# A decode layer: twelve down-projection chunks in one load, and TensorE's waits for itself moved to the other buffer

## The chip, the core and the metric

The kernel runs on one core of a Trainium2 chip. The core has five engines that run their own instruction streams: TensorE (PE; its weight loads are shown apart as PEld), VectorE (DVE), ScalarE (ACT), GpSimd (POOL) and SyncE (SP). Sixteen DMA engines carry data between HBM and the on-chip memory (SBUF). Engines tell one another through semaphores. The metric is the device time of one execution in microseconds (us), as the median of several runs. The profile is one more execution; its times are counted from the first instruction of the span.

## The reference

One token for each of eight sequences goes through an attention layer with a window of 1024 cached positions and a gated feed-forward layer, all in float32:

```python
h  = x + A(_layernorm(x))     # A: q = x @ wq; softmax(q k^T * Dh**-0.5) @ v over the last 1024
                              #    positions; 32 query heads on 4 key/value heads; then @ wo
h2 = h + B(_layernorm(h))     # B: (gelu(x @ w_gate) * (x @ w_up)) @ w_down
```

The width is 1024, the inner width of the feed-forward layer 3584. With eight tokens there is little arithmetic for each weight; weights and cache are 111 MB, and each byte is used once.

## The kernel before

**Stream.** All weights and both caches lie in HBM in the order in which they are used. SP issues them as one queue of loads into two SBUF buffers, `wbuf[0]` and `wbuf[1]`, each of 64 KB on each of the 128 partitions. Loads 0 to 11 fill one whole buffer each, in turn: 8 MiB, one row of 64 KB for each partition. Buffer 0 gets the even loads, buffer 1 the odd ones. `flow` lists them; `load(k, clear)` on L182 to L187 issues one, and L394 to L397 give each load its wait: the buffer has to be free, which TensorE tells by the semaphore `steps`.

**TensorE's loop.** TensorE runs a loop of stages. One pass is: eight transposes (`transposes`, L129), the sixteen products of buffer 0's first half, the sixteen of its second half, eight transposes, then the same two halves of buffer 1 (`products(i, half)`, L135 to L153). The text names these steps as the code does: t0, a0, a1, t1, b0, b1, with the pass in brackets, so b1(5) is the second half of buffer 1 in pass 5. There are passes 0 to 5, and pass 6 has t0, a0 and a1 alone. Each step ends by counting `steps` up by one. `pe(pass, step)` is the wait for that.

**One product** takes a 128x32 stationary tile and 512 columns of a weight row block. Its 32 outputs go to one of four strips of PSUM partitions (`j` = 0 to 3), and `c` = 0 to 3 accumulates. Products with different `j` can run side by side on the array; the profile has two MATMUL records for each product.

**The waits of TensorE for its own count.** In `products`, L150 to L152, TensorE counts up the semaphore `pace` with a product and at once waits for that count. So it waits until that product has ended before it begins the next. Before the change this is done in the second half of buffer 0, after the products 1, 3 and 5, in every pass.

**The end of the stream.** Load 11 carries the last up-projection columns and chunks 0 to 7 of the down projection (a chunk is 128 rows of `w_down`, 4 KB on each partition). Load 12 has chunks 8 to 15 in the first half of buffer 0 (32 KB rows), loads 13 and 14 have four chunks each in its second half (16 KB rows). Load 12 tells of its landing by the buffer's semaphore `landed[0]`; loads 13 and 14 have one of their own, and L418 and L419 let GpSimd pass each landing on to TensorE, as the release of products 0 to 7 and of 8 to 15 of a1(6). Two more loads bring chunks 24, 25 and chunk 26 into buffer 1, and two last ones chunk 27 in two column blocks (160 and 96 of each 256); they wait for b0(5) only.

**What is done with them.** b1(5) multiplies chunks 0 to 7, a0(6) chunks 8 to 15, a1(6) chunks 16 to 23. VectorE sums the parts in `d0` (L440, L442). TensorE then multiplies chunks 24 and 25 (L448), adds `d0` into the same accumulator by two constant matrices (L455), multiplies chunk 26, and ScalarE copies the sum to `s_sb` (L461). The two blocks of chunk 27 (L467) are added to it by VectorE (L470), and two DMAs store the result.

Of the kernel before, what the change touches and what calls it, by code (L numbers as in the profile page):

```python
# [10 lines left out]
D = 1024  # L11
# [5 lines left out]
NQ = 4  # L17
# [5 lines left out]
HALF = BUF // 2  # L23
# [2 lines left out]

LATE = (5, 6, 4)

PARTS = (8, 8, 4, 4, 2, 1)
ENDS = (160, 96)  # L30
SINGLES_AT, LAST = 24, 27

# [1 line left out]
class Flow:  # L34
# [38 lines left out]
    def run(self, engine, make, *waits, mark=True):  # L73
        ins = self.start(engine, make, waits)
        if not mark:
            return None
        self.done[engine] += 1
        ins.then_inc(self.own[engine], 1)
        return self.own[engine], self.done[engine]
# [6 lines left out]
    def go(self, engine, sem, n, *waits):  # L86

        self.start(engine, lambda e: e.sem_inc(sem, n), waits)


def decode_block(nc, x, flow, tail, outs):

    fl = Flow(nc)
    run, move, go = fl.run, fl.move, fl.go
# [18 lines left out]
    ready = [fl.sem("ga"), fl.sem("gb")]  # L113
# [5 lines left out]
    def pe(it, step):  # L119
        return steps, 6 * it + 1 + ("t0", "a0", "a1", "t1", "b0", "b1").index(step)  # L120
# [5 lines left out]
    def take(sem, n):  # L126
        t.wait_ge(sem, n).then_inc(sem, -n)  # L127
# [7 lines left out]
    def products(i, half):  # L135
        if half == 0:
            take(landed[i], 16)
        take(ready[i], 1)
        out = big[i][:, half * N:(half + 1) * N]
        for n in range(4 * NQ):  # L140
            c, j = divmod(n, NQ)
            if (i, half, n) == (0, 1, 8):
                take(ready[i], 1)
            s0 = (half * NQ + j) * WIN + 32 * c
            w0 = half * HALF + (c * NQ + j) * N
            ins = t.matmul(  # L146
                out[32 * j:32 * j + 32, :], st[i][:, s0:s0 + 32], wbuf[i][:, w0:w0 + N],
                start=(c == 0), stop=(c == 3))

            if (i, half) == (0, 1) and n in (1, 3, 5):  # L150
                ins.then_inc(pace, 1)
                take(pace, 1)  # L152
        ins.then_inc(steps, 1)  # L153
# [3 lines left out]
    with nc.body("stage", valid_engines=[PE]):  # L157
        back = t.mark_branch_hint_location()
        transposes()
        products(0, 0)  # L160
        products(0, 1)
        nc.br_cmp(count, 6, on_true="rest", on_false="down", comp_op="IS_LT", engines=[PE])
    with nc.body("rest", valid_engines=[PE]):
        transposes()
        products(1, 0)
        products(1, 1)
        t.reg_add(count, count, 1)
        t.br_lt(count, 7, on_true="stage", on_false="down").branch_hint(back)
# [13 lines left out]
    def load(k, *waits):  # L182
        i, a, src, own = flow[k]
        n = src.shape[1]
        s = fl.sem(f"part{k}") if own else landed[i]
        fl.start("sync", lambda e: e.dma_start(wbuf[i][:, a:a + n], src), waits).then_inc(s, 16)
        return s, 16  # L187
# [63 lines left out]
    def paired(engine, i, k, src, *waits):  # L251

        s = src.rearrange("p (c e) m -> p e c m", e=2)
        for e2 in range(2):
            tok = run(engine, lambda e: e.tensor_copy(  # L255
                windows(i)[:, k, 2 * e2:2 * e2 + 2].rearrange("p h (c m) -> p h c m", m=32),
                s[:, e2].unsqueeze(1).to_broadcast([P, 2, 4, 32])), *waits)
        return tok
# [6 lines left out]
    for hf in range(2):  # L265
# [9 lines left out]
        for s in range(2):  # L275
# [5 lines left out]
        fill = run("gpsimd", lambda e: e.tensor_copy(  # L281
            st[hf].rearrange("p (k n) -> p k n", k=2),
            qz[hf].unsqueeze(1).to_broadcast([P, 2, NQ * WIN])), tok, pe(0, end))
# [30 lines left out]
    for hf in range(2):  # L314
# [23 lines left out]
        for s in range(2):  # L338
            fill = paired("gpsimd", hf, s, ot[:, s * REP:(s + 1) * REP].rearrange(
                "p h b r -> p h (b r)"), tok, pe(2, ("a1", "b1")[hf]))  # L340
# [40 lines left out]
    fill = paired("gpsimd", 1, 0, xt.rearrange("p c b r -> p c (b r)"), b_free, pe(4, "b1"))  # L381
# [11 lines left out]
    arrived = {}  # L393
    for k in range(2, len(flow)):  # L394
        i, a, src, mine = flow[k]
        clear = pe(k // 2 - 1, ("a1", "b1")[i]) if k < 12 else pe(5, "a0" if k == 12 else "a1")
        arrived[k] = load(k, clear)  # L397

    fill = paired("gpsimd", 1, 1, at[:, 0:8], at_ok[0], b_free)
# [14 lines left out]
    fill = paired("gpsimd", 0, 0, at[:, 8:16], at_ok[0], a_free, pe(5, "a1"))  # L414
    go("gpsimd", ready[0], 1, fill)
    at_ok.append(to_chunks(16, len(LATE), pe(6, "t0")))
    fill = paired("gpsimd", 0, 1, at[:, 16:24], at_ok[1], pe(5, "a1"))
    for k in (13, 14):  # L418
        go("gpsimd", ready[0], 1, fill, arrived[k])  # L419


    later = wbuf[1][:, 0:HALF]
# [2 lines left out]
    for k, src in enumerate(tail[:-len(ENDS)]):  # L425
        n = src.shape[1] // D
# [129 lines left out]
```

## Time and profile before

| | before |
|---|---|
| median of 3 runs | 264.21 us (264.13 to 264.34) |
| the profiled execution | 263.94 us |
| its span, first to last instruction | 262.6 us |
| PE busy / PEld busy | 152.1 us / 51.7 us |
| DVE, ACT, POOL busy | 34.7, 16.6, 16.0 us |
| DMA | 111.31 MB, mean 424 GB/s over the span |
| mean granted TensorE clock | 0.825 |

The profiled execution is 1.3 us longer than its span, for what lies around the first and the last instruction. In the rows that follow, a row of the timeline is: start, duration, engine, line, operation, tiles, shapes, count, and in brackets the idle time before it. A row of the waits or of the DMA issues names the engine that waits or issues. A "q" behind an engine (SPq, PEq) is its sequencer.

### The profile page before, as it was taken

To read this page: it belongs to the slowest core of one execution; us is meant where nothing else is said; L and a number is where in the kernel's file an instruction comes from. 1 tells how busy PE (TensorE), PEld (TensorE's weight loads), DVE (VectorE), ACT (ScalarE), POOL (GpSimd) and SP (SyncE) were. 2 spreads that over 40 slices of the span, in tenths; PEclk is the share of its full clock that TensorE was granted. 3 is DMA by queue.
4 is the path that set the end of the run, shared out by engine and by line. 5 is a ranking of instruction groups with operands and counts; after the bars stand their busy time and mean duration, and the time that the engine had idled before them with its cause. 6 is when DMAs were issued, how large, how long until landed. Compare 5 with 4: busy or idle time off the path is not lost. (4 is left out here: it accounts for less than half of the span.)

```text
span 262.6 us, 2312 instructions
## 1 busy us (share of the span) xinstructions
PE 152.1 (58%) x984; PEld 51.7 (20%) x984; DVE 34.7 (13%) x78; ACT 16.6 (6%) x25; POOL 16.0 (6%) x31
## 2 busy tenths in 40 slices
PE   0024955805937827917618928429909609809976
PEld 0021221301222222212112212122302202302312
DVE  0220010100021110040310020730100300201211
ACT  1000000000030020000000000300200000000000
POOL 5020010010000000020020000020000110100100
PEclk9999995975975956995975977956985967977999
DMA  8998997999899799989979998997999899799995
GB/s 319 484 419 379 479 479 329 469 479 429 369 479 479 339 459 479 439 359 479 479 329 469 479 429 369 479 479 329 469 479 439 359 479 479 329 464 404 422 417 220
DMA packets 3056, 111.31 MB, mean 424 GB/s; under 512 B 480, under 2 KB 736, under 8 KB 1008
## 3 DMA queue, kind: packets, MB, share of 16 engines
q1 hardware_dynamic: 2880, 111.23, 98.4%
q10 hardware_dynamic: 176, 0.08, 0.1%
HBM read 111.18 MB, written 0.13 MB: 424 GB/s over the span
## 5 line engine op out<-in xcount | busy, mean ns | idle before, releaser
L146 PE MATMUL big<-w,st 128*32 128x512 f32 x832 | 132.2, 720 | 73.8 <-PEq L127 72.1
L146 PEld LDWEIGHTS big<-w,st 128*32 128x32 f32 x832 | 36.4, 129 | 161.4 <-issue 158.9
L132 PE MATMUL tp<-ident,tin 128*128 128x128 f32 x104 | 17.5, 323 | 34.2 <-PEq L127 34.2
L132 PEld LDWEIGHTS tp<-ident,tin 128*128 128x128 f32 x104 | 14.0, 166 | 44.5 <-issue 44.5
L255 POOL COPY st<-ot 128x256 f32<-128x256 f32 x8 | 2.9, 400 | 77.1 <-DVE ot L334 77.1
L293 DVE TENSOR_REDUCE nmax<-big 128x1 f32<-128x1024 f32 x2 | 2.4, 1224 | 30.7 <-PE big L146 30.7
L246 POOL COPY st<-xt 128x1024 f32<-128x1024 f32 x2 | 3.0, 1524 | 52.2 <-DVE xt L241 52.2
L271 DVE TENSOR_TENSOR tin<-big,q 128x512 f32<-128x512 f32 x2 | 1.4, 692 | 31.3 <-PE big L146 31.3
L319 DVE TENSOR_TENSOR o<-big,o 128x512 f32<-128x512 f32 x2 | 1.4, 692 | 28.6 <-PE big L146 28.6
L255 POOL COPY st<-at 128x256 f32<-128x256 f32 x6 | 2.8, 494 | 36.0 <-DVE at L385 18.5
L281 POOL COPY st<-qz 128x1280 f32<-128x1280 f32 x2 | 2.5, 1254 | 34.1 <-DVE qz L276 34.1
L270 ACT COPY q<-big 128x512 f32<-128x512 f32 x2 | 1.2, 586 | 34.5 <-PE big L146 34.5
L255 POOL COPY st<-xt 128x256 f32<-128x256 f32 x2 | 1.3, 660 | 31.8 <-DVE us L377 31.8
L348 DVE TENSOR_TENSOR y<-big,y 128x512 f32<-128x512 f32 x1 | 0.7, 692 | 18.4 <-PE big L146 18.4
L318 ACT COPY o<-big 128x512 f32<-128x512 f32 x2 | 1.2, 585 | 28.9 <-PE big L146 28.9
L404 DVE TENSOR_TENSOR gs<-big,gs 128x512 f32<-128x512 f32 x1 | 0.7, 691 | 17.4 <-PE big L146 17.4
L295 ACT ACTIVATE tin<-big,nmax 128x1024 f32<-128x1024 f32 x2 | 2.2, 1114 | 11.9 <-DVE nmax L293 11.9
L295 ACT ACT_TABLE_LOAD x1 | 1.3, 1283 | 26.8 <-DVE nmax L293 26.8
L226 ACT ACT_TABLE_LOAD x2 | 2.6, 1283 | 1.9 <-POOL ident L197 1.9
L442 DVE TENSOR_TENSOR d<-big,d 128x512 f32<-128x512 f32 x2 | 1.4, 692 | 9.5 <-PE big L146 9.5
L373 DVE TENSOR_TENSOR gs<-big,gs 128x512 f32<-128x512 f32 x1 | 0.7, 692 | 14.6 <-PE big L146 14.6
L403 ACT COPY gs<-big 128x512 f32<-128x512 f32 x1 | 0.6, 585 | 30.6 <-PE big L146 30.6
(69 smaller groups left out, 42.4 us busy)
## 6 DMA issues: line engine op xcount, KB each, us to landing
w<-weights SPq DMA_DIRECT2D x1, 4096.0 KB, 23.7
w<-weights SPq DMA_DIRECT2D x2, 2048.0 KB, 24.7
w<-weights SPq DMA_DIRECT2D x1, 1024.0 KB, 16.1
w<-weights SPq DMA_DIRECT2D x1, 512.0 KB, 17.0
w<-weights SPq DMA_DIRECT2D x1, 320.0 KB, 17.3
w<-weights SPq DMA_DIRECT2D x12, 27.9
w<-weights SPq DMA_DIRECT2D x1, 192.0 KB, 17.3
out<-o_fin SPq DMA_DIRECT2D x1, 80.0 KB, 1.7
```

What stands on the lines that cost most here:

```text
L132: ins = t.transpose(tp[:, i * P:(i + 1) * P], tin[:, i * P:(i + 1) * P], ident)
L146: ins = t.matmul(out[32 * j:32 * j + 32, :], st[i][:, s0:s0 + 32], wbuf[i][:, w0:w0 + N], start=(c == 0), stop=(c == 3))
L226: tok = run("scalar", lambda e: e.activation(sd, ve, AF.Sqrt), tok)
L246: fill = run(engine, lambda e: e.tensor_copy(windows(i), half.unsqueeze(2).to_broadcast([P, 2, NQ, 4 * 32])), tok, *clear)
L255: tok = run(engine, lambda e: e.tensor_copy(windows(i)[:, k, 2 * e2:2 * e2 + 2].rearrange("p h (c m) -> p h c m", m=32), s[:, e2].unsqueez ...
L270: tok = run("scalar", lambda e: e.copy(q_sb, w0), pe(0, ("a0", "b0")[hf]))
L271: tok = run("vector", lambda e: e.tensor_add(tin[:, 0:N], w1, q_sb), tok, pe(0, end), pe(0, ("t0", "t1")[hf]))
L281: fill = run("gpsimd", lambda e: e.tensor_copy(st[hf].rearrange("p (k n) -> p k n", k=2), qz[hf].unsqueeze(1).to_broadcast([P, 2, NQ * WIN ...
L293: tok = run("vector", lambda e: e.tensor_reduce(out=nmax, in_=s_ps, axis=AX.X, op=ALU.max, negate=True), pe(1, ("a1", "b1")[hf]))
L295: p_ok = run("scalar", lambda e: e.activation(tin, s_ps, AF.Exp, bias=nmax, accum_out=tot), tok, pe(1, ("t0", "t1")[hf]))
L319: tok = run("vector", lambda e: e.tensor_add(o_sb, big[hf][:, N:2 * N], o1), tok, pe(2, ("a1", "b1")[hf]))
L442: tok = run("vector", lambda e: e.tensor_add(d0, ya[:, k], d0), tok, pe(6, f"a{k}"))
```

## The change

Three things are done. The row blocks of the down projection are cut into parts of 8, 12, 4, 2 and 1 chunks in place of 8, 8, 4, 4, 2 and 1: chunks 8 to 19 come as one load of 48 KB rows, which covers the first half of buffer 0 and half of its second half. This load waits for a1(5), as the next one does, where the old load 12 waited for a0(5) alone. The release of products 0 to 7 of a1(6) no longer waits for a landing of its own. And TensorE's waits for its own count are taken out of the second half of buffer 0 and put into the second half of buffer 1, after the products 1, 3, 5, 7, 9, 11 and 13: seven in each of passes 0 to 5, where there were three in each of passes 0 to 6.

```diff
-PARTS = (8, 8, 4, 4, 2, 1)
+PARTS = (8, 12, 4, 2, 1)
...
-            if (i, half) == (0, 1) and n in (1, 3, 5):
+            if (i, half) == (1, 1) and n % 2 == 1 and n < 4 * NQ - 1:
                 ins.then_inc(pace, 1)
                 take(pace, 1)
...
-        clear = pe(k // 2 - 1, ("a1", "b1")[i]) if k < 12 else pe(5, "a0" if k == 12 else "a1")
+        clear = pe(k // 2 - 1, ("a1", "b1")[i]) if k < 12 else pe(5, "a1")
...
-    for k in (13, 14):
-        go("gpsimd", ready[0], 1, fill, arrived[k])
+    go("gpsimd", ready[0], 1, fill)
+    go("gpsimd", ready[0], 1, fill, arrived[13])
...
-    flow += [(0, HALF + m * 4 * D, srcs[13 + m], True) for m in range(2)]
-    decode_block(nc, x=aps["x"], flow=flow, tail=srcs[15:], outs=outs)
+    flow.append((0, HALF + 4 * D, srcs[13], True))
+    decode_block(nc, x=aps["x"], flow=flow, tail=srcs[14:], outs=outs)
```

TensorE's rows for the second half of buffer 0, as the difference has them ("ga" is the semaphore that releases buffer 0's products, "pace" the one for TensorE's own count):

```order
 L146 MATMUL big<-w,st 32x512 x15
 L146 MATMUL big<-w,st 32x512 [waits ga_done]
-L146 MATMUL big<-w,st 32x512
-L146 MATMUL big<-w,st 32x512 [waits pace_done]
-L146 MATMUL big<-w,st 32x512
-L146 MATMUL big<-w,st 32x512 [waits pace_done]
-L146 MATMUL big<-w,st 32x512
-L146 MATMUL big<-w,st 32x512 [waits pace_done]
-L146 MATMUL big<-w,st 32x512
+L146 MATMUL big<-w,st 32x512 x7
 L146 MATMUL big<-w,st 32x512 [waits ga_done]
 L146 MATMUL big<-w,st 32x512 x7
```

The three waits are gone; the wait for the release of the last eight products stays where it was.

The end of TensorE's loop before, from the last fifteen products of b0 on ("gb" releases buffer 1's products; L167 and L168 count the pass and branch back):

```order
L146 MATMUL big<-w,st 32x512 x15
L146 MATMUL big<-w,st 32x512 [waits gb_done]
L146 MATMUL big<-w,st 32x512 x15
L167 REGISTER_ALU
L168 COMPARE_AND_BRANCH
```

The last seven rows of the same place now:

```order
L146 MATMUL big<-w,st 32x512
L146 MATMUL big<-w,st 32x512 [waits pace_done]
L146 MATMUL big<-w,st 32x512
L146 MATMUL big<-w,st 32x512 [waits pace_done]
L146 MATMUL big<-w,st 32x512
L167 REGISTER_ALU
L168 COMPARE_AND_BRANCH
```

These are the last two of the seven waits; the fifteen products that ran without one now go two at a time, up to the branch.

SP's queue before, from load 2 on ("steps" is TensorE's count of finished steps; a row without a wait follows a row that has waited for the same):

```order
L186 DMA w<-weights 128x16384 [waits steps_done] x10
L186 DMA w<-weights 128x8192 [waits steps_done]
L186 DMA w<-weights 128x4096 [waits steps_done]
L186 DMA w<-weights 128x4096
L83 DMA w<-weights 128x2048 [waits steps_done]
```

And now:

```order
L186 DMA w<-weights 128x16384 [waits steps_done] x10
L186 DMA w<-weights 128x12288 [waits steps_done]
L186 DMA w<-weights 128x4096
L83 DMA w<-weights 128x2048 [waits steps_done]
L83 DMA w<-weights 128x1024
```

One load fewer is issued, and the remaining one of 128x4096 no longer has a wait of its own, since the load ahead of it already waits for a1(5).

## The prediction

> **What bounds the kernel now.** I read the DMA queues first, since the kernel uses each byte once, then the windows in time order, the chain that ended last, and the timeline of TensorE from the landing of load 11 on.
>
> ```profile
> span 262.6 us, 2312 instructions
> q1 hardware_dynamic: 2880, 111.23, 98.4%
> 40.00:80.00 40.00, 22.87 (x144) 7.97 (x144) 3.12 (x7) 3.52 (x5) 1.25 (x1) 0.76 1.00 431
> 234.00:258.00 24.00, 20.02 (x143) 5.70 (x147) 3.90 (x6) 1.17 (x2) 1.14 (x2) 0.88 0.97 414
> 235.89 5.64 PE big L146 x32
> 242.39 17.33 DMA w<-weights
> ```
>
> In the windows the last two numbers are the DMA engines' share and GB/s. SP's one queue is busy for 98.4% of sixteen engines' span. It runs at 431 GB/s in mid kernel and at 414 at the end, where rows get short; there are no pauses to win back. In the chain the last 17.33 us before the final products are the queue's. So time goes only if the stream or the little behind it gets shorter. It comes if the stream stops, or if TensorE is still at work when the last bytes land. The second is the question here.
>
> **TensorE beside the end of the stream, before.**
>
> ```profile
> 235.89 9.03 PE L146 MATMUL big<-w,st 128*32 128x512 f32 x64 [7.11 <-PEq L127]
> 244.85 1.09 PE L132 MATMUL tp<-ident,tin 128*128 128x128 f32 x8
> 245.87 3.64 PE L146 MATMUL big<-w,st 128*32 128x512 f32 x32
> 250.43 1.05 PE L146 MATMUL big<-w,st 128*32 128x512 f32 x4 [0.92 <-PEq L127]
> 251.63 1.05 PE L146 MATMUL big<-w,st 128*32 128x512 f32 x4
> ...
> 255.30 1.92 PE L146 MATMUL big<-w,st 128*32 128x512 f32 x16 [0.21 <-PEq L127]
> 257.74 1.07 PE L448 MATMUL acc<-w,at 128*32 128x256 f32 x16 [0.52 <-DMA w<-weights]
> 258.60 0.64 PE L448 MATMUL acc<-d,add 128*32 128x256 f32 x8
> 259.03 0.64 PE L448 MATMUL acc<-w,at 128*32 128x256 f32 x8
> ```
>
> In order: b0(5) with b1(5), t6, a0(6), the paced pairs of a1(6), its second half, then the final chunks. TensorE waits between them: 0.92 us for load 13, 0.21 for load 14, 0.52 for chunks 24 and 25. That is its spare time.
>
> **Price of a self-wait.** Two products between waits come every 251.63 - 250.43 = 1.20 us. Unpaced products:
>
> ```profile
> 241.30 0.14 PEld L146 LDWEIGHTS big<-w,st 128*32 128x32 f32 x4 [0.29 <-issue]
> 241.73 0.14 PEld L146 LDWEIGHTS big<-w,st 128*32 128x32 f32 x4 [0.29 <-issue]
> ```
>
> Four records, which are two products, go every 0.43 us. So a wait costs 1.20 - 0.43 = 0.77 us of TensorE: two strips of the array stand empty.
>
> **Part 1, waits out of buffer 0.** Three waits go in each pass: 3 x 0.77 = 2.3 us earlier at the end of a1. Passes 1 to 6 gain that only on TensorE. The next thing a1 releases is a load that queues behind the other buffer's.
>
> **Part 2, waits into buffer 1.** Before, b1(5) has eight groups from 241.30 on, the last at 241.30 + 7 x 0.43 = 244.31, and ends at 235.89 + 9.03 = 244.92. Now its last pair begins at 241.30 + 7 x 1.20 = 249.70 and ends at 250.75. So b1 ends 5.8 us later, in each of passes 0 to 5. Two things are behind it in TensorE's queue: t0 of the next pass, and a0 behind that. SP's next odd load waits for it too.
>
> *Does the stream stop?* The closest odd loads:
>
> ```profile
> 206.85 0.33 SPq L186 DMA_DIRECT2D w<-weights  x1
> 189.65 0.33 SPq L186 DMA_DIRECT2D w<-weights  x1
> w<-weights SPq DMA_DIRECT2D x1, 26.6
> out<-o_fin SPq DMA_DIRECT2D x1, 80.0 KB, 1.7
> ```
>
> Load 11, issued at 206.85, would go at 212.65. Load 10 ahead of it lands at 189.65 + 26.6 = 216.25. How long an issue takes to bring its first bytes isn't shown for a large load. It is above zero, and at most 1.7 us by the nearest row, an idle queue's store from issue to landing. I take 1.7; that leaves 3.6 - 1.7 = 1.9 us, so I cost it at nothing. The other odd loads are issued at the same place of a pass. If the cover were gone, each us beyond it would cost one us in each of five passes.
>
> *Do the passes fall behind?* The dependent step closest to its landing is a0(4), behind the second layer norm, t0(4) and VectorE's fill:
>
> ```profile
> 174.34 0.69 DVE L246 COPY st<-xt 128x1024 f32<-128x1024 f32 x1
> 177.84 1.08 PE L146 MATMUL big<-w,st 128*32 128x512 f32 x4 [4.06 <-PEq L127]
> ```
>
> The fill ends at 175.03 + 5.8 = 180.8, so a0(4) begins 3.0 us late, and a1(4) gets 2.3 back. Load 10 goes at 189.65 + 0.7 = 190.4. Its 8.4 MB take 19.5 us at 431 GB/s, so load 9 has the queue until 216.25 - 19.5 = 196.8. Hidden.
>
> *At the end it is not hidden.* b1(5) starts after load 11's landing, which nothing here moves. So:
> - t6 begins at 244.85 + 5.8 = 250.7, a0(6) at 251.7.
> - a0(6) and a1(6) run without waits: sixteen groups of 0.43, and 0.63 more for the last one (3.64 - 7 x 0.43): 251.7 + 15 x 0.43 + 0.63 = 258.8. Before, a1(6) ended at 255.30 + 1.92 = 257.2. It ends **1.55 us later**, after the three waits of a1(6) have been given back.
>
> ```profile
> 246.60 1.14 POOL L255 COPY st<-at 128x256 f32<-128x256 f32 x2 [17.06 <-DVE at L385]
> 257.28 0.69 DVE L442 TENSOR_TENSOR d<-big,d 128x512 f32<-128x512 f32 x1 [7.01 <-PE big L146]
> 259.73 0.37 ACT L461 COPY s_sb<-acc 128x256 f32<-128x256 f32 x1 [14.16 <-PE acc L448]
> 260.38 0.33 DVE L470 TENSOR_TENSOR o_fin<-yt,s_sb 128x160 f32<-128x160 f32 x1 [2.40 <-PE yt L467]
> ```
>
> - a1(6)'s stationary tiles, filled by POOL, would be ready at 247.74 + 5.8 = 253.6; a1(6) needs them at 255.1. Hidden.
> - L442's second addition begins at 258.85 and ends at 259.54, so the products with `d0` begin at 259.6 in place of 258.60: 1.0 us late. Chunks 24 and 25 go ahead of them, from 258.6 to about 259.5, so they don't bind.
> - Chunk 26 follows 0.43 later and ends at 260.67; `s_sb` is there at 260.73 + 0.37 = 261.1. The final addition begins at 261.15 in place of 260.38. **The end moves by 0.75 us.** The rest of the one us was spare time between `s_sb` and the products of chunk 27.
>
> **Part 3, one load for twelve chunks.**
>
> ```profile
> 221.63 0.33 SPq L186 DMA_DIRECT2D w<-weights  x1
> w<-weights SPq DMA_DIRECT2D x1, 4096.0 KB, 23.7
> 227.78 0.81 SPq L186 DMA_DIRECT2D w<-weights  x2
> w<-weights SPq DMA_DIRECT2D x1, 2048.0 KB, 22.4
> w<-weights SPq DMA_DIRECT2D x2, 2048.0 KB, 24.7
> ```
>
> Eight chunks used to land at 221.63 + 23.7 = 245.3, the next four at 227.78 + 22.4 = 250.2, the last four about five us later, at 255.2 (2 x 24.7 - 22.4 = 27.0 behind the second issue). No row shows a 48 KB load. Its landing lies between 245.3 and 255.2; I take 250.2, when the same bytes were there before. a0(6) now waits for all twelve, but TensorE comes at 251.7, so 1.5 us of cover are left. If it landed at 255.2, a0(6) would start 3.5 us later still, and the kernel end near 268.5. The issue moves from 221.63 to about 225.5 (227.78 less 2.3), ten us ahead of load 11's landing. Fewer rows can speed the stream up: between nothing and what lifts 414 GB/s to 431 over these 8.4 MB, 0.8 us. I take 0.1, as a third of the rows go and they stay long; the end of the kernel does not see it, since TensorE is late.
>
> **Sum.** 263.94 + 0.75 = 264.7 for the profiled execution. This lies 0.27 below the median of the runs, so 264.21 + 0.75 = **264.95** against the median.
>
> **The clock makes this end uncertain.**
>
> ```profile
> 236.00:238.00 2.00, 2.00 (x12) 0.54 (x15) 0.00 (x0) 0.00 (x0) 0.00 (x0) 0.50 0.95 410
> 238.00:240.00 2.00, 2.00 (x12) 0.45 (x8) 0.00 (x0) 0.00 (x0) 0.00 (x0) 0.53 1.18 508
> 240.00:242.00 2.00, 2.00 (x24) 0.68 (x20) 0.00 (x0) 0.45 (x1) 0.00 (x0) 1.00 0.88 377
> 252.00:254.00 2.00, 1.73 (x8) 0.17 (x4) 0.00 (x0) 0.00 (x0) 0.00 (x0) 1.00 1.00 426
> 44.00:46.00 2.00, 2.00 (x18) 0.60 (x14) 0.00 (x0) 0.00 (x0) 0.00 (x0) 0.67 0.38 164
> 200.00:204.00 4.00, 4.00 (x28) 1.02 (x24) 0.58 (x1) 0.00 (x0) 0.00 (x0) 0.71 1.21 524
> 42.38 8.51 PE L146 MATMUL big<-w,st 128*32 128x512 f32 x64 [4.97 <-PEq L127]
> ```
>
> The third number from the end is the granted clock. At half clock 12 records go in 2 us, at full clock 24. In b(5) the clock rises at 239.9 (0.53 in its window), 4.0 us after the first product. In b(0) it rises 2.9 us after it (0.67 between 44 and 46, start 42.38); in b(4) 5.1 us after it (0.71 between 200 and 204: 202.3; b(4) starts where b(5) does, 38.7 us earlier). One us later costs half a us. Before, the 0.92 us ahead of a1(6) took that up; now it reaches the end. So the forecast's own spread is 0.75 - 0.55 to 0.75 + 0.55: 264.4 to 265.5.
>
> The Trainium skill, "TensorE: Matmul & The Clock Gate", Part 1, says the activity window is free-running, so the moment of the rise differs from run to run. By it the runs of the changed kernel would spread over the 1.1 us above; were the window tied to the kernel's start, each would take 264.95. The trace agrees as far as one run can: the three stages have 2.9, 4.0 and 5.1 us.
>
> **Rivals.**
> - *The end is not reached (not slower).* TensorE spends a wait more cheaply, or an early clock rise gives it 0.5 us and the spare time behind a1(6) the rest. It decides at 255.2, load 14's landing: if TensorE reaches the ninth product of a1(6) by then, and not at 256.9, nothing moves, 264.2. Against it: the pairs between 250.43 and 254 all keep 1.20 us. For it: only 0.2 us are left with the earliest clock rise.
> - *The clock falls in the paced half.* Pairs fill half the array. Were it to fall half way through b1(5), four pairs take 0.85 more each (two groups at half speed), and a0(6) starts at half clock for some 3 to 4 us, 1.5 to 2 us more: 264.7 + 5, near 270. Against it: the clock stays 1.00 over 252 to 254, where nothing but paced pairs runs. For it: that stretch is 5 us long, b1's is 9.
> - *The stream stops at odd loads*, if an issue needs more than 3.6 us to bring bytes: at one us over, five passes cost 5 us, 269 or more.
> - *The stream gets shorter (faster).* With 0.8 us won by the longer rows and TensorE early as in the first rival: 263.4.
>
> The same page, "A second HAM failure mode: psum-queue depth-cycling", says that short idle gaps between groups of matmuls can make the clock swing between half and full rate. That is the second rival; by the rule the time is near 270, by the row of 252 to 254 it is 264.95, and the row decides.
>
> **Chances and range.** The forecast has 0.76, the first rival 0.12, the clock 0.05, the stopped stream 0.03, the shorter stream 0.04. About 0.2% (0.53 us) is what a measurement here can tell from no change. The forecast's spread of 264.4 to 265.5 has seven parts in ten above 264.74: 0.53 slower, 0.23 same. With the rivals: slower 0.61, same 0.35, faster 0.04. Range: from the first rival's time, 264.1, to the forecast's upper end and 0.2 for the landing of the 48 KB rows, 265.7. The clock, the stopped and the shorter stream stay outside, 0.12.
>
> **What would show it.** After: eight pairs in b1(5), 1.20 us apart; t6 near 250.7; no wait of TensorE for a landing from there to chunk 27; L442's second addition near 258.9; the stream's share and landings as before. The step fails if a0(6) is seen waiting for load 12, if the clock shows 0.50 inside a b1, or if an odd load is issued after its predecessor has landed.

## The result, and the profile after

| | before | changed |
|---|---|---|
| median | 264.27 us (264.08 to 264.50, 6 runs) | 267.12 us (266.35 to 270.07, 6 runs) |
| ratio | | 1.0127, 95% interval 1.0078 to 1.0175 |
| the profiled execution, its span | 263.94, 262.6 | 267.32, 266.0 |

Slower, as forecast, but by 2.85 us where 0.75 was forecast; the time lies outside the range of 264.1 to 265.7. The runs also spread over 3.7 us, where those of before spread over 0.4. Of all runs below, one counts as slow, at over 1.5% above the fastest of its kernel, and is left out.

The page of the changed kernel; the third line is the chain that ended last, by engine:

```profile
span 266.0 us, 2332 instructions
...
q1 hardware_dynamic: 2736, 111.23, 97.3%
...
PE 4%; DVE 0%; issue 0%
```

The chain that ended last holds no DMA any more. From the last pair of b1(5) on, TensorE and the additions behind it set the end, which was the forecast's mechanism. The timeline of TensorE, from b0(5) on:

```profile
237.88 8.23 PE L146 MATMUL big<-w,st 128*32 128x512 f32 x40 [10.11 <-PEq L127]
...
249.87 3.46 PE L146 MATMUL big<-w,st 128*32 128x512 f32 x12
253.26 1.09 PE L132 MATMUL tp<-ident,tin 128*128 128x128 f32 x8
254.28 7.07 PE L146 MATMUL big<-w,st 128*32 128x512 f32 x64
261.17 1.05 PE L448 MATMUL acc<-w,at 128*32 128x256 f32 x16
262.26 0.64 PE L448 MATMUL acc<-d,add 128*32 128x256 f32 x8
```

No bracket stands behind the transposes: TensorE waits for no landing there. From t6 to the products with `d0` it takes 262.26 - 253.26 = 9.0 us; the forecast had 250.7 to 259.6, 8.9. So the steps of the end are right, and all of them are 2.6 us later than forecast. Of this, 2.0 us are there before b(5) begins: its first product starts at 237.88 and not at 235.89, since load 11 lands late. SP's timeline of the changed kernel at loads 10 and 11, and beneath it their times from issue to landing:

```profile
192.79 0.33 SPq L186 DMA_DIRECT2D w<-weights  x1
213.22 0.33 SPq L186 DMA_DIRECT2D w<-weights  x1
```

```profile
w<-weights SPq DMA_DIRECT2D x1, 24.9
w<-weights SPq DMA_DIRECT2D x1, 24.4
```

Load 10 lands at 217.7, load 11 at 237.6. Before, load 10 landed at 216.25, and load 11, issued at 206.85, took this from issue to landing:

```profile
w<-weights SPq DMA_DIRECT2D x1, 28.8
```

So it landed at 206.85 + 28.8 = 235.65. The issue of load 11 is at 213.22, near the 212.65 of the forecast. All odd loads, read in the same two views:

| odd load | issued | predecessor lands | lead | lands | later than before |
|---|---|---|---|---|---|
| 3 | 56.63 | 61.5 | 4.9 | 80.8 | 0.0 |
| 5 | 96.45 | 100.2 | 3.7 | 120.25 | 0.75 |
| 7 | 134.94 | 139.6 | 4.7 | 158.9 | 0.7 |
| 9 | 174.77 | 178.3 | 3.5 | 198.3 | 1.4 |
| 11 | 213.22 | 217.7 | 4.5 | 237.6 | 2.0 |

Lateness grows at loads 5, 9 and 11, those with the shortest leads, and nothing brings it back. The trace also holds every single packet with its start and duration, which the views print only as sums, and there the dry queue can be seen. Around the landings ahead of loads 5, 9 and 11, the time in which one of the sixteen DMA engines has no packet of the stream adds up to 1.4, 1.9 and 2.2 us; around the other landings, and around all of them before, it is under 0.1 us. One engine ends load 4 at 99.18 and gets its first packet of load 5 at 100.56, 4.1 us after the issue. The first packets of these three loads also take up to 3.2, 3.2 and 3.8 us, where 2.42 is usual.

The remaining 0.6 us is the clock. The windows of the changed kernel in b(5):

```profile
240.00:242.00 2.00, 2.00 (x12) 0.46 (x8) 0.00 (x0) 0.00 (x0) 0.00 (x0) 0.50 1.02 442
242.00:244.00 2.00, 2.00 (x18) 0.66 (x12) 0.00 (x0) 0.00 (x0) 0.00 (x0) 0.74 0.91 393
244.00:252.00 8.00, 7.10 (x32) 1.04 (x25) 1.37 (x2) 0.58 (x1) 0.00 (x0) 1.00 0.95 410
```

The clock rises at 243.0 (0.74 between 242 and 244), 5.2 us after the first product; half of 5.2 - 4.0 is 0.6 us. In the paced half, b1(5), it stays at 1.00. So the profiled execution adds up: 262.6 + 2.0 (landing of load 11) + 0.6 (clock) + 0.75 (end) = 265.95, measured 266.0.

### The profile page after: what moved, and what is told of

Same layout as the page of the kernel before. It is cut to its first block, busy times and chain, and to the rows that moved or that the text cites. A ratio compares the mean times of both kernels' runs of the same rounds, so it can differ in the third digit from the quotient of the medians.

```text
span 266.0 us, 2332 instructions
## 1 busy us (share of the span) xinstructions
PE 163.4 (61%) x984; PEld 50.1 (19%) x984; DVE 34.6 (13%) x78; ACT 16.6 (6%) x25; POOL 16.0 (6%) x31
## 5 line engine op out<-in xcount | busy, mean ns | idle before, releaser
L146 PE MATMUL big<-w,st 128*32 128x512 f32 x832 | 144.6, 721 | 66.1 <-PEq L127 59.9
L146 PEld LDWEIGHTS big<-w,st 128*32 128x32 f32 x832 | 35.1, 128 | 167.4 <-issue 167.4
L132 PE MATMUL tp<-ident,tin 128*128 128x128 f32 x104 | 16.9, 316 | 34.1 <-PEq L127 34.1
L132 PEld LDWEIGHTS tp<-ident,tin 128*128 128x128 f32 x104 | 13.4, 161 | 44.5 <-issue 44.5
L295 ACT ACT_TABLE_LOAD x1 | 1.3, 1283 | 23.9 <-DVE nmax L293 23.9
L411 DVE TENSOR_TENSOR us<-big,top 64x512 f32<-64x512 f32 x1 | 0.7, 683 | 15.6 <-ACT top L410 15.6
L351 DVE TENSOR_TENSOR lo<-big,y 64x512 f32<-64x512 f32 x1 | 0.7, 682 | 15.1 <-PE big L146 15.1
L385 DVE COPY at<-tp 128x512 f32<-128x512 f32 (+1 forms) x2 | 1.2, 625 | 9.5 <-PE tp L132 9.5
L355 ACT COPY top<-big 64x512 f32<-64x512 f32 x1 | 0.6, 582 | 28.6 <-PE big L146 28.6
```

The source lines that it names most:

```text
L132: ins = t.transpose(tp[:, i * P:(i + 1) * P], tin[:, i * P:(i + 1) * P], ident)
L146: ins = t.matmul(out[32 * j:32 * j + 32, :], st[i][:, s0:s0 + 32], wbuf[i][:, w0:w0 + N], start=(c == 0), stop=(c == 3))
L295: p_ok = run("scalar", lambda e: e.activation(tin, s_ps, AF.Exp, bias=nmax, accum_out=tot), tok, pe(1, ("t0", "t1")[hf]))
```

## The experiments

**Theories.** A: the seven waits release buffer 1 so late that the stream runs dry at the odd loads; what it loses stays lost, and the late end comes on top. B: only the end counts, and load 11's late landing is chance. C: the load of 48 KB rows costs the time. D, put up after the first four runs: the paced products themselves slow the DMA, whenever the loads are issued. Each run has its own runs of the kernel before beside it, with medians from 263.95 to 264.04, and a single run of 264.16 for the last three. A diff shows the lines that matter; "..." stands for others.

**The merge without any waits.**

```diff
-            if (i, half) == (1, 1) and n % 2 == 1 and n < 4 * NQ - 1:
-                ins.then_inc(pace, 1)
-                take(pace, 1)
```

> The twelve-chunk load as in the change, and no waits of TensorE for itself at all. Theory A (the seven waits release buffer 1 so late that the stream runs dry at the odd loads; load 11 lands 2.0 us late, and the waits of pass 5 put 0.75 us and the clock's phase on top): load 11 lands at 235.6 as before, a0(6) begins at 250.2 when load 12 lands, time 264.2 (264.0 to 264.4). Theory B (only the end counts: the waits of pass 5; the rest is chance): 264.2 too. Theory C (the load of 48 KB rows costs the time): 266 or more.

Measured: 265.44 us, ratio 1.0058 (1.0038 to 1.0077). No theory had this time. The timeline of this kernel, and its clock:

```profile
245.03 1.09 PE L132 MATMUL tp<-ident,tin 128*128 128x128 f32 x8
250.39 8.77 PE L146 MATMUL big<-w,st 128*32 128x512 f32 x64 [4.27 <-PEq L127]
258.95 1.07 PE L444 MATMUL acc<-w,at 128*32 128x256 f32 x16
```

```profile
250.00:252.00 2.00, 1.61 (x12) 0.59 (x16) 0.00 (x0) 0.00 (x0) 0.00 (x0) 0.65 1.09 467
252.00:254.00 2.00, 2.00 (x16) 0.68 (x12) 0.00 (x0) 0.00 (x0) 0.00 (x0) 0.50 0.96 410
```

Load 12 lands at 250.1, as the forecast took it, and load 11 at 235.5. But TensorE has now waited 4.27 us for it, its clock falls just as a0(6) begins (0.65 and 0.50 in the two windows), and a0(6) and a1(6) take 8.77 us where the changed kernel takes 7.07 from a full clock. So the merge is not harmless by itself; theory C in its own form, a slow load, is not what happens.

**The move without the merge**, that is, the kernel before with only the condition of the waits exchanged:

```diff
-            if (i, half) == (0, 1) and n in (1, 3, 5):
+            if (i, half) == (1, 1) and n % 2 == 1 and n < 4 * NQ - 1:
```

> The kernel before, with only the waits moved from the second half of buffer 0 to that of buffer 1 (three become seven); the loads stay as they were. Theory A: as the changed kernel, 266.3 to 268.5, load 11 landing near 237.6. Theory B: the same time. Theory C: 264.3.

Measured: 266.62 us (265.23 to 267.28), ratio 1.0093 (1.007 to 1.0116). The move alone is about as slow as the change. That speaks against C. In its profiled execution load 11 lands at 212.16 + 24.0 = 236.2, 0.6 us late, less than the 2.0 that was expected; that execution took 265.93 us, less than the median.

**Waits in some passes only, by a branch.** TensorE's loop gets a second copy of b1, and a branch on the pass chooses.

```diff
...
-        products(1, 1)
+        nc.br_cmp(count, 5, on_true="loop", on_false="last", comp_op="IS_LT", engines=[PE])
+    with nc.body("loop", valid_engines=[PE]):
+        products(1, 1, paced=False)
...
+    with nc.body("last", valid_engines=[PE]):
+        products(1, 1, paced=True)
...
```

> The changed kernel with the seven waits in pass 5 alone (a branch in TensorE's loop chooses between two copies of b1). Theory A: the odd loads are issued as early as before, load 11 lands at 235.6, and only the end is late: 264.95, 264.4 to 265.5 with the clock's phase. Theory B: as the changed kernel, 267.

Measured: 267.71 us. The opposite choice:

> The changed kernel with the seven waits in passes 0 to 4 and none in pass 5. Theory A: load 11 lands some 2 us late (237 to 238), everything behind it in the queue as well, so the last block lands near 262 in place of 260.2: 266.1, 265.2 to 267. Theory B: 264.2, load 11 at 235.6.

Measured: 269.02 us (268.05 to 271.78). Both are spoiled by something else. TensorE's timeline in the first of them, at the products of chunk 27:

```profile
261.13 0.43 PE L473 MATMUL yt<-w,at 128*32 128x160 f32 x2
263.93 0.34 PE L473 MATMUL yt<-w,at 128*32 128x160 f32 x3 [2.37 <-issue]
```

Between two products with the same operands TensorE stands still for 2.37 us, and nothing in the profile releases it. The other kernel has 2.50 us at the same place; no kernel with the shorter loop has it. That the longer program is the cause is likely, but wasn't tried. Up to there the first of them fits theory A: load 11 at 235.6, the products with `d0` at 260.27 with the clock's rise at 241.0 (5.1 us after the first product, 0.55 us), against 259.6 forecast. In the second, load 11 lands at 214.28 + 24.1 = 238.4, 2.8 us late, where theory A had some 2 us and B none.

**The same without a longer program.** GpSimd adds seven to `pace` at the start, so that every wait passes at once, and takes them away before pass 5:

```diff
+    go("gpsimd", pace, 7)
     t.reg_mov(count, 0)
...
+    go("gpsimd", pace, -7, b_free)
     fill = paired("gpsimd", 1, 1, at[:, 0:8], at_ok[0], b_free)
```

> The seven waits bind in pass 5 alone, with TensorE's program word for word that of the change: GpSimd adds seven to the count at the start, so the waits pass at once, and takes the seven away before pass 5. Theory A (an odd load has to be issued some 4.5 us before its predecessor lands; the seven waits take that lead away; what the stream loses stays lost): stream as before, load 11 lands at 235.6, only the end is late: 264.95, 264.4 to 265.5 with the clock's phase. Theory D (the paced products themselves slow the DMA, whenever the loads are issued): load 11 still at 235.6, the loads behind it later, 265.5 or more.

Measured: **265.05 us** (264.57 to 266.06, 7 runs), ratio 1.0042 (1.0026 to 1.0058). The late end alone costs 1.0 us in the median, with 0.75 forecast. D is not borne out: what lands behind load 11 is as late as load 11 itself, 0.35 us, and no later. The timeline of this kernel:

```profile
236.28 6.01 PE L146 MATMUL big<-w,st 128*32 128x512 f32 x36 [8.66 <-PEq L127]
...
250.63 1.09 PE L132 MATMUL tp<-ident,tin 128*128 128x128 f32 x8
...
259.63 0.64 PE L450 MATMUL acc<-d,add 128*32 128x256 f32 x8
```

t6 at 250.63 and the products with `d0` at 259.63 were forecast at 250.7 and 259.6. Here the landing of load 11 is 0.35 us late and the clock rises early, 3.1 us after the first product, which takes 0.45 off.

**All passes but the last**, with the seven added before pass 5 in place of the two lines above:

> The opposite: the seven waits bind in passes 0 to 4; before pass 5 GpSimd adds seven to the count and b1(5) runs freely. Theory A: load 11 lands 1 to 3 us late; b1(5) ends early, TensorE then idles over 4 us for load 12, its clock falls, and a0(6) begins at half clock: 267.4, 266 to 268.5. Without that idling it would be 266.1.

Measured: 266.02 us (265.55 to 267.46, 5 runs; a sixth, the one left out, took 269.83), ratio 1.0091 (1.0069 to 1.0112). As expected the stream's loss and the idle clock add up: in the profiled execution load 11 lands at 236.25, 0.65 us late, TensorE waits 4.54 us for load 12, and its clock falls to 0.50. The time alone does not decide against B, since the merge without any waits, with the same idle clock, took 265.44 and the intervals of the two ratios overlap. What speaks against chance is where load 11 is late. It lands 0.6 to 2.8 us late in all five profiled executions in which the seven waits bind in passes 0 to 4 and the odd loads go whole (the change twice, the move alone, and the two kernels with waits in all passes but the last). In the eight of the other experiments with the merged load it is at most 0.4 us late.

**The late release undone, all seven waits kept.** Each odd load is cut in two; the first half goes when b0 has ended, so the queue has work while b1 is paced.

```diff
...
-        fl.start("sync", lambda e: e.dma_start(wbuf[i][:, a:a + n], src), waits).then_inc(s, 16)
+        cuts = [(0, HALF), (HALF, BUF)] if i else [(0, n)]
+        for (c0, c1), w in zip(cuts, waits or (None, None)):
+            fl.start("sync", lambda e: e.dma_start(wbuf[i][:, a + c0:a + c1], src[:, c0:c1]),
+                     [w]).then_inc(s, 16)
...
-        arrived[k] = load(k, clear)
+        arrived[k] = load(k, *([pe(k // 2 - 1, "b0"), clear] if i else [clear]))
```

> The changed kernel with each odd load cut into two, the first half issued when b0 has ended and only the second when b1 has; all seven waits stay. Theory A: the queue never runs dry, load 11 lands at 235.6 to 235.8, and what is left is the late end: 264.95, 264.4 to 265.5. Theory D: as the changed kernel, near 267, load 11 near 237.6.

Measured: 265.43 us (265.03 to 265.82, 6 runs), ratio 1.0047 (1.0035 to 1.006). The waits are the same as in the changed kernel, only the issue is earlier: 1.7 us come back, and the spread shrinks from 3.7 to 0.8 us. Theory D falls. The second half of load 11, by SP's timeline and the issues:

```profile
212.01 0.33 SPq L188 DMA_DIRECT2D w<-weights  x1
```

```profile
w<-weights SPq DMA_DIRECT2D x1, 4096.0 KB, 24.0
```

It lands at 212.01 + 24.0 = 236.0, 0.4 us late, more than was expected; the loads are cut into more rows here, but what the 0.4 us are wasn't tried.

**Fewer waits.** `n < 11` in place of `n < 4 * NQ - 1`:

> The changed kernel with five waits in place of seven. b1 ends 3.9 us later than unpaced (5 x 0.77), so odd loads are issued some 2 us earlier than with seven. Theory A: no loss in the stream or at most 0.2, load 11 at 235.6 to 235.8; t6 begins near 249, TensorE idles about 1 us before load 12 lands and keeps its clock: 264.2, 264.0 to 264.6. Theory D: five sevenths of the loss of the stream stay, 265.5 or more.

Measured: **264.00 us** (263.85 to 264.37, 11 runs), ratio 1.0001 (0.9992 to 1.0009). The timeline of this kernel:

```profile
249.64 1.09 PE L132 MATMUL tp<-ident,tin 128*128 128x128 f32 x8
250.66 7.07 PE L146 MATMUL big<-w,st 128*32 128x512 f32 x64
257.68 1.07 PE L448 MATMUL acc<-w,at 128*32 128x256 f32 x16
258.64 0.64 PE L448 MATMUL acc<-d,add 128*32 128x256 f32 x8
```

a0(6) begins half a us after load 12 has landed, and the products with `d0` at 258.64, as before (258.60). Load 11, issued at 209.92, has a lead of 6.4 us and lands at 235.6. With six waits (`n < 13`) and with three (`n in (1, 3, 5)`):

> The changed kernel with six waits. Theory A: odd loads are issued about 0.8 us earlier than with seven, 4.5 to 5.5 us before their predecessors land: a loss of 0 to 0.4 in the stream; t6 near 250, so the end is late by 0 to 0.5: 264.4, 264.0 to 265.2.

> The changed kernel with three waits, after products 1, 3 and 5 of b1. Theory A: no loss in the stream; t6 ends near 248.5, TensorE idles 1.7 us before load 12 lands, against 4.3 us without waits; if the clock holds over that, 264.1 (263.9 to 264.4), if it falls as it did without waits, near 265.4.

Measured: 264.04 us (263.64 to 264.50, 12 runs), ratio 0.9998 (0.9989 to 1.0006), and 263.88 us (263.75 to 264.73, 11 runs), ratio 1.0000 (0.9991 to 1.0009). Three, five and six waits all give the time of before, so the loss begins between six and seven. With six, the odd loads have leads of 4.4 to 5.7 us, against 3.5 to 4.8 with seven; load 11 lands 0.3 us late, and the products with `d0` begin at 259.00. With three waits TensorE idles 0.79 us before a0(6) by its timeline and keeps its clock.

**The merge with the waits of before** (`(0, 1) and n in (1, 3, 5)`):

> The twelve-chunk load with the waits where they were before (three in the second half of buffer 0). TensorE idles over 4 us before load 12, its clock falls, a0(6) begins at half clock as in the run without waits, and the three waits of a1(6) put 2.3 us on top, with nothing behind to take it up: 267.7, 267 to 268.5. If the merge were harmless with the old waits: 264.2.

Measured: 268.03 us (266.2 to 268.99), ratio 1.0149 (1.012 to 1.0178). The idle clock of the merge and the three waits of a1(6) add up to about what was worked out.

**Late odd loads alone.** The kernel before, TensorE's program untouched:

```diff
-        clear = pe(k // 2 - 1, ("a1", "b1")[i]) if k < 12 else pe(5, "a0" if k == 12 else "a1")
+        clear = pe(k // 2 - 1, "a1") if k % 2 == 0 and k < 12 else pe(k // 2, "t0") if k < 12 else pe(5, "a0" if k == 12 else "a1")
```

> The kernel before, with TensorE and its waits untouched; only the odd loads 3 to 11 wait for t0 of the next pass in place of b1, which puts their issue 2 to 7 us later. Theory A: load 9 is then issued some 3.7 us before load 8 lands and load 5 some 4.7 us before load 4; the others keep 6 us or more. Load 9 loses 0.2 to 1.3 us, load 5 up to 0.3, and all landings behind are late by the sum: 264.3 to 265.6. If it is something TensorE does and not the time of the issue: 264.0, like before.

Measured: 265.51 us (263.9 to 266.31, 6 runs), ratio 1.0061 (1.0044 to 1.0078). The late issue is enough to lose time. The one execution of these that has a profile took 263.9 and lost nothing, so the kernel was run and profiled twice more:

> The kernel before with odd loads waiting for t0 of the next pass, once more. Theory A: where the run takes more than 264.5, load 11 or the loads behind it land late by the same amount, and the first late landing is one of an odd load issued less than 5 us before its predecessor landed (5 or 9). Otherwise: load 11 at 235.6 and the time lost behind it.

> The same kernel and the same expectation as the run just before it.

Measured: 266.58 and 265.94 us, the kernel before beside them 264.16. Load 9 of the first of these, by SP's timeline and the issues:

```profile
175.81 0.33 SPq L186 DMA_DIRECT2D w<-weights  x1
```

```profile
w<-weights SPq DMA_DIRECT2D x1, 23.7
```

It was issued 2.2 us before load 8 landed (151.81 + 26.2 = 178.0) and lands at 199.5, against 196.9 before. Around the landing of load 8 the engines have no packet for 5.2 us in sum. The timeline of TensorE at the end of the same execution:

```profile
253.12 1.05 PE L146 MATMUL big<-w,st 128*32 128x512 f32 x4 [0.54 <-PEq L127]
...
260.43 1.07 PE L448 MATMUL acc<-w,at 128*32 128x256 f32 x16 [0.52 <-DMA w<-weights]
```

TensorE waits for landings just as in the kernel before, only 2.7 us later: the time is lost in the stream. In the second one load 9 lands at 175.30 + 23.5 = 198.8. Load 8 is 0.45 us late in both already, so load 9 itself loses 2.2 and 1.4 us, more than the 0.2 to 1.3 us that were expected. In the execution of 263.9 us it was issued 3.0 us ahead, no engine was without a packet, and nothing was lost.

**The changed kernel once more.**

> The changed kernel once more. Theory A: its span is 262.6 + 0.75 + (landing of load 11 less 235.6) + half of (the clock's rise after b(5)'s first product less 4.0), to within 0.2 us; the landing 1 to 3 us late, lost at odd loads issued less than 5 us before their predecessors landed.

Measured: 268.2 us, span 266.8. Load 11 lands at 214.16 + 23.9 = 238.1, 2.4 late; the clock rises 5.9 us after b(5)'s first product, 0.95: 262.6 + 0.75 + 2.4 + 0.95 = 266.7. The same sum for the kernel with the waits in pass 5 alone gives 262.6 + 0.75 + 0.35 - 0.45 = 263.25, measured 263.4; for the split loads 262.6 + 0.75 + 0.35 + 0.65 = 264.35, measured 264.5 (its clock rises 5.3 us after the first product). With the one of the result these are four executions, each within 0.15 us.

## Why the prediction was wrong

- **What bounds the kernel: right.** The last landing set the end before, TensorE does in the changed kernel.
- **The price of a self-wait (0.77 us) and b1's late end (5.8 us): right.** In the changed kernel the last three pairs of b1(5), of four records each, begin at 249.87, and t6 follows 3.39 us later: two periods of 1.20 and 0.99 for the last pair.
- **The sum of the end, 0.75 us: right in its steps.** Where the loads are issued as before it is 265.05 us against 264.04; the profiled steps agree to 0.1 us. The rest of the 1.0 us may be what the clock and a late landing of load 11 make of it from run to run; only one of the seven runs has a profile.
- **"I take 1.7; that leaves 3.6 - 1.7 = 1.9 us, so I cost it at nothing": the step that failed.** The loss of the stream was put at nothing and measured 2.0 us in the profiled execution. The row behind it, a store of 80 KB on an idle queue that takes 1.7 us from issue to landing, was no upper bound for a load of 128 rows of 64 KB: one engine got its first packet 4.1 us after the issue. Of the odd loads that were issued 2.2 to 4.5 us before their predecessors landed, many came late by 0.2 to 2.2 us each, others by less or not at all; with 4.6 us or more none lost over 0.2 us. In the medians this is some 1.8 us of the 2.85, since the waits in pass 5 alone cost 1.0; the ratios, 1.0127 and 1.0042, lie 0.85% apart. The rival "the stream stops at odd loads" had been given 0.03, and its price of five us for five passes was too large, since only some of the loads lose time.
- **The landing of the 48 KB load at 250.2: right** (250.1 to 250.2 where the stream was on time). That "the cover" of the merge is TensorE's paced work was seen, but what is lost without it was not: TensorE idles, and its clock falls.
- **The clock.** The spread of 2.9 to 5.1 us for its rise was too narrow: 2.9 to 5.9 were seen in b(5). The second rival, a fall of the clock in the paced half, did not happen: 1.00 from 244 to 262. The Trainium skill, "TensorE: Matmul & The Clock Gate", "A second HAM failure mode: psum-queue depth-cycling", has short idle gaps between groups of matmuls throw the clock back; gaps of 0.15 us do not do it here. Its Part 1 has the clock fall after an idle window of about 3.4 us: that agrees with 4.27, 4.44, 4.54 and 5.01 us of waiting for load 12, after which it fell, and with 0.79 us, after which it did not.

Why an issue needs so long a lead is open. On the idle queue at the start, the sixteen engines get their first packets of load 0 1.0 to 1.6 us after its issue; in mid stream it took up to 4.1 us. What SP does in between is not in the trace. Why the same lead sometimes costs nothing is open too: in the execution of 263.9 us all sixteen had their first packet of load 9 within 2.7 us. And short leads are not the only source of small losses: with the waits in all passes but the last, load 4 lost 0.35 us with a lead of 10.3 us.

No version beat the kernel before. With three, five and six waits the merged load ties with it. With three the last landing sets the end again: the queue is back in the chain that ended last. With five and six that chain is TensorE's, but level with the landings; with five, chunk 27's first block lands at 259.66 and its products begin at 259.70.

## What to carry to other kernels

In a kernel that lives on one stream of loads, the release of a buffer is the event to guard: measure how long before the end of its predecessor each load is issued, and treat a lead that no row of the profile has shown as a risk, not as cover. Slowing an engine that is off the path is free only up to that lead, and lost time in the stream adds up from load to load. Work that fills a wait can keep the clock up, but an end that hangs on a half-clock start varies from run to run.

## What the runs showed of the hardware

- In this stream of 8 MiB loads an odd load was safe when it was issued 4.6 us or more before the current one landed (at most 0.2 us lost); leads of 2.2 to 4.5 us cost 0 to 2.2 us for each load. In mid stream an engine's first packet of a new load came up to 4.1 us after the issue (load 5 of the changed kernel), against 1.0 to 1.6 us on the idle queue (load 0 before).
- Time that the stream loses stays lost: in the changed kernel the lateness of the odd loads goes 0.0, 0.75, 0.7, 1.4, 2.0 us.
- A wait of TensorE of 4.27 to 5.01 us just ahead of sixteen plus sixteen products made them 1.45 to 2.7 us longer (8.52 to 9.75 us against 7.07); the granted clock is 0.50 in the first 3.0 to 5.4 us of them.
- A second copy of sixteen products and a branch in TensorE's program went with a stall of 2.4 to 2.5 us among its last products.
